# Moving the flips of the gate sums behind the next sums in a fused attention and mixture-of-experts kernel

## The chip, the cores and the metric

The kernel runs on one core of a Trainium2 chip. The metric is the device time of one execution in microseconds (us). The engines are named PE (TensorE, with its weight loads as PEld), DVE (VectorE), ACT (ScalarE), POOL (GpSimd) and SP (SyncE). Each takes its own queue in order.

## The reference

Attention over 8 batches, 12 heads, 448 tokens and 64 dimensions, with capped scores, and then a mixture of 8 experts with one expert for each token:

```python
scores = scale * np.matmul(q, k.transpose(0, 1, 3, 2))
scores = cap * np.tanh(scores / cap)
attn = np.exp(scores - max); attn = attn / (sum(attn) + 1e-09)
x = matmul(attn, v)                                   # 3584 tokens x 768
e_idx = np.argmax(x @ w_gate + modality_bias[modality_id], axis=1)
out[mask] = gate_w[mask, None] * (np.maximum(x[mask] @ w1[e], 0.0) @ w2[e])   # for each expert e
```

(The lines on the softmax and the experts are shortened.)

## The kernel before

The attention runs over 24 **units**, three to a batch; a unit is four heads of one batch. A unit has seven **steps** of 64 keys. The loop in `attention` goes over all 168 steps and writes the order of each engine by hand.

A step has on PE a group of eight score matmuls (L542, tile `sc`, two buffers) and a group of eight that weigh the values with an earlier step's probabilities (L574, tile `xT`, one buffer); each group works on four 64x64 tiles of the array. ACT takes the tanh of a step's scores (L547) and, after every second step, two exponentials (L549). So ACT's order is tanh, tanh, exp, exp. A scores group for step n writes the buffer that the tanh of step n-2 has read, so it waits for that tanh. DVE adds the probabilities up (L562, `tot`) and, once a unit's last step is weighed (which falls in step 3 of the next unit), copies `xT` out of PSUM (L581); the next unit's first weighing waits for that copy. It stands on PE in step 6 of an even unit and in step 5 of an odd unit, counted by the unit that is then being scored.

Two units, an even unit a and a+1, make a **pair**, and every 14 steps have some further work on PE for a pair:

- **sums** (`sums2`, L613 and L615, tile `glog`): softmax denominators and gate logits, sixteen recorded matmuls on 128x32 tiles of the array, in step 5 of an even unit; DVE copies them to `gl` (L619).
- **flip** (`turn2` calls `flip`, L604, tile `lt`): four 128x128 transposes of `gl`, in step 4 of the odd unit that follows, six steps after the sums; DVE then takes reciprocals (L632) into the batch's **payload** `pay`, and `logits` multiplies (L655).

When a batch's third unit has its logits, `start_route` begins its **route**: a chain of small DVE operations (L286 to L340), one small exponential on ACT, two small rank matmuls on PE, and then indirect DMAs from POOL (L346) that write payload rows to a map in DRAM. `go_on` moves a route on at given steps. The PE operations and the large DVE and ACT operations are pinned in the written order; most of the route's DVE operations aren't, and a scheduler places them. The payload of a batch has a buffer by its number modulo two.

After the loop come the closing sums and the experts' layers, in which PE multiplies almost without a break; their first expert needs the map, which is complete for all but the last batch some two units before the loop's end.

The lines that the change touches are in `payload` and `attention`:

Of the kernel before, what the change touches and what calls it, by code (L numbers as in the profile page):

```python
# [39 lines left out]
F32 = mybir.dt.float32  # L40
# [10 lines left out]
C, CP = 4, 112  # L51
# [13 lines left out]
ENTRY = 16  # L65
# [17 lines left out]
NU = NP // 2  # L83
ND = NU * B
PAIRED = ND - 4
LAGS = ((5, 5, 5, 5, 4, 4, 3), (6, 5, 5, 5, 4, 4, 4))
PLAGS = ((6, 6, 5, 5, 5, 4, 4), (5, 5, 5, 5, 4, 4, 4))
LAST = (4, 4, 4, 4, 4, 4, 4)
# [4 lines left out]
class Program:  # L93
# [7 lines left out]
    def pin(self, inst):  # L101
        return self.tc.keep_in_program_order(inst)
# [156 lines left out]
    def payload(self, b, pool, tok=None):  # L259

        nc = self.nc
        pay = pool.tile([CP, C, ENTRY], F32, name="pay" if tok is not None else f"pay{b % 2}")
        if tok is None:
            nc.gpsimd.memset(pay, 0.0)
            nc.gpsimd.iota(pay.bitcast(I32)[:, :, 0], pattern=[[CP, C]], base=b * S, channel_multiplier=1)
            nc.gpsimd.iota(
                pay[:, :, FOUR::SEG], pattern=[[Q * CP, C], [0, 2]], base=Q * b * S, channel_multiplier=Q,
                allow_small_or_imprecise_dtypes=True,
            )
        else:  # L270
            nc.gpsimd.memset(pay, 1.0)
            nc.vector.tensor_copy(pay.bitcast(I32)[:, :, 0], tok)
            for j in range(2):
                nc.vector.tensor_scalar(pay[:, :, FOUR + j * SEG], tok, float(Q), None, op0=ALU.mult)
        return pay
# [232 lines left out]
    def attention(self, firsts, rp, xp):  # L508
        tc, nc = self.tc, self.nc
        pe, pin, V = nc.tensor, self.pin, nc.vector  # L510
        with ExitStack() as st:
# [10 lines left out]
            def fetch(d):  # L522
                if d < ND:
                    for g in (2 * d, 2 * d + 1) if d else ():
                        self.load_kq(ring[g % 4], g)
                    vas[d] = ld.tile([128, VW], F32, name="va")
                    self.load(vas[d], self.v[d // NU, d % NU])
# [73 lines left out]
            def flip(gl, bank=None):  # L601
                bank = bank or self.ps_r.tile([128, 512], F32, name="lt", tag="small")
                for c in range(C):
                    pin(pe.transpose(bank[:CP, c * 128 : (c + 1) * 128], gl[:, c * CP : (c + 1) * CP], self.ident))  # L604
                return bank[:CP].rearrange("p (c g x) -> p c g x", c=C, g=4)

            def sums2(a, copy=V.tensor_copy):

                glog = self.glog = ps_g.tile([128, 512], F32, name="glog", tag="glog")
                group = lambda x: glog[x * GW : (x + 1) * GW, :S]  # L610
                every = [(u, g) for u in range(2) for g in range(2)]
                for u, g in every:
                    pin(pe.matmul(group(2 * u + g), self.pick2, tots[a + u][:, g], start=True, stop=False))  # L613
                for u, g in every:
                    pin(pe.matmul(  # L615
                        group(2 * u + g), self.wgt[:, (2 * (a + u) + g) % NP], kept[a + u][:, g], start=False, stop=True
                    ))
                gls[a] = xp.tile([128, S], F32, name="gl", bufs=2)
                pin(copy(gls[a], glog[:, :S]))  # L619

            def recs(d):

                b, r = divmod(d, NU)
                if r == 0:
                    pays[b] = self.payload(b, rp)
                return self.recips(pays[b])[:, :, :, 2 * r : 2 * r + 2]

            def turn2(a):

                lt = flip(gls.pop(a))  # L630
                for u in range(2):
                    pin(V.reciprocal(recs(a + u), lt[:, :, 2 * u : 2 * u + 2, GE : GE + 2]))  # L632
                    lts[a + u] = lt[:, :, 2 * u : 2 * u + 2]
# [12 lines left out]
            def logits(d):  # L646

                b, r = divmod(d, NU)
                lt = lts.pop(d)
                rec = self.recips(pays[b])  # L650
                if r == 0:
                    lgs[b] = xp.tile([CP, C, H, E], F32, name="lg", bufs=2)
                for i in range(2):
                    h0 = 4 * r + 2 * i
                    pin(V.tensor_tensor(  # L655
                        lgs[b][:, :, h0 : h0 + 2], lt[:, :, i, :GE].rearrange("p c (j e) -> p c j e", j=2),
                        rec[:, :, :, 2 * r + i].unsqueeze(3).to_broadcast([CP, C, 2, E]), op=ALU.mult,
                    ))
# [31 lines left out]
            def go_on():  # L690
                for way in routing:
                    next(way, None)
# [15 lines left out]
            for m in range(END):  # L708
                d, s = divmod(m, STEPS)
                due[min(m + (LAST if d == ND - 1 else (PLAGS if d < PAIRED else LAGS)[d % 2])[s], END)].append(m)  # L710
            added, held = 0, range(STEPS * (SOON + 2), STEPS * (SOON + 2) + 5)
# [12 lines left out]
            for n in range(END):  # L724
                d, s = divmod(n, STEPS)
                if s == 0:
                    fetch(d + 1)
                    if 1 < d < SOON and d % NU == 1:
                        store(d // NU - 1)
                    if d == 0:  # L730
                        self.fetch_bias()
                        self.fetch_cap()
                    if d == 1:
                        self.blank(xp.tile([128, FF], F32, name="spare", bufs=2))
                    if 0 <= d - 2 < CLEAR:
                        self.empty_map(d - 2)
                scores(n)
                late = False
                if not late:
                    more(n)  # L740
                if (d, s) == (1, 3):
                    self.gate_bias()
                if (d, s) == (1, 4):
                    self.columns()
                if s == 1 and d % 2 == 0 and self.rest:
                    self.rest.pop()()
                if s in ((1,), (1, 6))[d % 2] and d != SOON + 2:
                    go_on()
                if s == 4 and d % 2 and 3 <= d < PAIRED + 3:
                    turn2(d - 3)  # L750
                    go_on()
                    logits(d - 3)
                    logits(d - 2)
                if s == 5 and d % 2 == 0 and 2 <= d <= PAIRED:
                    sums2(d - 2)
                if (d, s) == (SOON + 1, 5):
                    sums(SOON)
                if s == 5 and d % 2 and 3 <= d < PAIRED + 2:
                    for u in (d - 3, d - 2):
                        if u % NU == NU - 1:  # L760
                            start_route(u // NU)
                if (d, s) == (SOON + 2, 2):
                    more(n, 1)
                for m in due[n]:
                    weigh(m)
                    if m % STEPS == STEPS - 1:
                        keep(m // STEPS)
                if s == 3 and d % 2 == 0 and d != SOON + 2:
                    go_on()
                if s == (2 if d % 2 else 4) and d % NU == 2:  # L770
                    tokens(d - 2)
                if s == (4 if d == SOON + 1 else 6) and 0 < d < ND - 1 and d % NU != 1:
                    tokens(d - 1)
                    if d == SOON + 1:
                        store(d // NU - 1)
                if d == SOON + 2 and s in (3, 4):
                    more(n, {3: 2, 4: 9}[s])
                if (d, s) == (SOON + 1, 6):
                    turn(SOON)
                    logits(SOON)  # L780
                    start_route(SOON // NU, firm=True)
                    go_on()
                    go_on()
                if (d, s) == (SOON + 2, 1):
                    go_on()
                    meta = self.early_slot(self.cpool, self.ps_r)
                    self.first_e = self.expert(meta, 0)
                    load_w1((0, 1), self.first_e)
                if (d, s) == (SOON + 2, 4):
                    maps = self.rows(meta, 0)  # L790
                    got = self.gather(maps, known=NT - S)
                    load_w1((2, 3, 4, 5), self.register(nc.gpsimd, meta[0:1, 0:1], E - 1, got.ins), nc.gpsimd)
                if d == SOON + 3 and s >= STEPS - TW:
                    self.norm(maps, s - (STEPS - TW))
# [818 lines left out]
```

## Time and profile before

| | us |
|---|---|
| median of 3 runs (lowest, highest) | 791.64 (791.25, 797.95) |
| the profiled execution, device time | 786.07 |
| its span, first to last instruction | 784.5 |
| mean granted TensorE clock of the span | 0.998 |

| engine | busy in the span |
|---|---|
| PE | 98% |
| DVE | 67% |
| ACT | 64% |
| POOL | 30% |

The busy shares are means over two very different stages. In the attention, which takes some 300 us, PE and ACT are both busy nearly all the time; in the experts' layers PE alone is. In the page's 40 slices ACT has a nine in slices 2 to 14, and three to six tenths from slice 17 to 39.

### The profile page before, as it was taken

How to read it: one execution, taken by the hardware profiler on the slowest of the kernel's cores; microseconds unless marked ns; L12 is line 12 of the kernel's file. 1: busy time of each engine (PE TensorE's matmuls, PEld its weight loads, DVE VectorE, ACT ScalarE, POOL GpSimd, SP SyncE). 2: the span in 40 equal slices, each digit the busy share in tenths (PEclk: the TensorE clock that was granted, in tenths of full speed). 3: DMA queues.
4: the chain of work that ended last, by engine and by line, in shares of the span. 5: the costliest groups of instructions: out<-in, count | busy, mean ns of one | idle time of the engine just before them, and what ended most of it. 6: DMA issues, size and time to landing. Idle time of an engine off the chain costs nothing. (4 is left out here: it accounts for less than half of the span.)

```text
span 784.5 us, 15421 instructions
## 1 busy us (share of the span) xinstructions
PE 772.2 (98%) x5811; PEld 580.0 (74%) x5811; DVE 524.3 (67%) x899; ACT 500.0 (64%) x704; POOL 238.4 (30%) x259
## 2 busy tenths in 40 slices
PE   7999999999999999999999999999999999999996
PEld 2343333343333337999999999999999999998985
DVE  4778897888798898965826448265482664727830
ACT  7999999999999895454533445235443354436630
POOL 3000121022122140248560723607427064015202
PEclk9999999999999999999999999999999999999999
DMA  6366545262544664598444563455634655346772
GB/s 201 115 205 204 163 144 182 102 213 94 192 141 146 165 219 154 141 311 277 157 138 176 191 229 131 142 202 185 201 124 157 228 174 183 109 176 207 244 283 98
DMA packets 58951, 139.33 MB, mean 178 GB/s; under 512 B 9025, under 2 KB 25814, under 8 KB 58867
## 3 DMA queue, kind: packets, MB, share of 16 engines
q1 hardware_dynamic: 48512, 113.32, 44.3%
q0 software_dynamic: 10352, 24.94, 9.4%
q8 instruction: 47, 0.77, 0.4%
q14 instruction: 38, 0.30, 0.1%
q10 hardware_dynamic: 2, 0.00, 0.0%
HBM read 114.47 MB, written 24.34 MB: 177 GB/s over the span
## 5 line engine op out<-in xcount | busy, mean ns | idle before, releaser
L549 ACT ACTIVATE pt<-pt 128x896 f32<-128x896 f32 x168 | 152.2, 972 | 0.0
L547 ACT ACTIVATE pt<-sc 128x896 f32<-128x896 f32 x164 | 145.6, 938 | 9.9 <-PE sc L542 9.6
L574 PE MATMUL xT<-pt,va 64*64 64x448 f32 x1344 | 149.8, 537 | 0.1
L1111 PE MATMUL py<-bh,hh 128*128 128x384 f32 (+1 forms) x440 | 147.9, 336 | 0.1
L1111 PE MATMUL py<-bh,hl 128*128 128x384 f32 (+1 forms) x440 | 147.5, 335 | 0.0
L1111 PE MATMUL py<-bl,hh 128*128 128x384 f32 (+1 forms) x440 | 147.5, 335 | 0.0
L1054 PE MATMUL ph<-x,al 128*128 128x384 f32 (+1 forms) x456 | 147.3, 323 | 0.0
L957 POOL DMA_INDIRECT xg<-xd,at x92 | 112.3, 1221 | 112.1 <-DVE look L1275 85.0
L562 DVE TENSOR_TENSOR tot<-tot,pt 128x896 f32<-128x896 f32 x118 | 127.8, 1083 | 9.2 <-ACT pt L549 3.4
L1050 PE MATMUL ph<-x,ah 128*128 128x384 f32 x360 | 120.6, 335 | 0.0
L1051 PE MATMUL ph<-x,ah 128*128 128x384 f32 x360 | 120.3, 334 | 0.0
L346 POOL DMA_INDIRECT mapd<-pay,pos x32 | 39.8, 1245 | 244.7 <-DVE pos L340 128.6
L574 PEld LDWEIGHTS xT<-pt,va 64*64 64x64 f32 x1344 | 51.1, 133 | 75.5 <-issue 70.8
L995 DVE TENSOR_TENSOR bl<-raw,bh 128x768 fp32r<-128x768 f32 x78 | 72.2, 955 | 39.8 <-ACT bh L994 39.5
L1133 ACT ACTIVATE ot<-py,mt 128x384 f32<-128x384 f32 (+1 forms) x55 | 31.9, 581 | 104.7 <-PE py L1111 93.8
L1054 PEld LDWEIGHTS ph<-x,al 128*128 128x128 f32 x456 | 85.7, 188 | 0.0
L1065 ACT ACTIVATE hh<-ph 128x384 fp32r<-128x384 f32 x63 | 30.6, 489 | 84.9 <-PE ph L1054 80.7
L1111 PEld LDWEIGHTS py<-bh,hh 128*128 128x128 f32 x440 | 82.6, 188 | 1.2 <-ACT ot L1133 0.5
L1111 PEld LDWEIGHTS py<-bl,hh 128*128 128x128 f32 x440 | 82.6, 188 | 0.3
L1111 PEld LDWEIGHTS py<-bh,hl 128*128 128x128 f32 x440 | 82.6, 188 | 0.3
L542 PE MATMUL sc<-kq 64*64 64x448 f32 x672 | 78.3, 551 | 4.0 <-ACT pt L547 4.0
L542 PE MATMUL sc<-kx 64*64 64x448 f32 x672 | 78.5, 540 | 0.1
(245 smaller groups left out, 972.9 us busy)
## 6 DMA issues: line engine op xcount, KB each, us to landing
raw<-in_w_dram SPq DMA_DIRECT2D x81, 384.0 KB, 4.7
raw<-in_w_dram SPq DMA_DIRECT2D x48, 512.0 KB, 4.5
va<-in_v_dram SPq DMA_DIRECT2D x24, 448.0 KB, 5.7
kx<-in_kq_dram SPq DMA_DIRECT2D x24, 448.0 KB, 3.8
xd<-xs SPq DMA_DIRECT2D x32, 336.0 KB, 6.8
kq<-in_kq_dram SPq DMA_DIRECT2D x22, 448.0 KB, 4.0
raw<-in_w1q_dram SPq DMA_DIRECT2D x12, 512.0 KB, 7.6
mapd<-spare SPq DMA_DIRECT2D x4, 480.0 KB, 8.1
```

What stands on the lines that cost most here:

```text
L346: put = nc.gpsimd.indirect_dma_start(self.mapd, bass.IndirectOffsetOnAxis(ap=pos, axis=0), pay[:, c, :], None, bounds_check=E * RG - 1, oo ...
L542: pin(pe.matmul(sc[i * KB : (i + 1) * KB, j, :S], kq[rows, S + s * KB : S + (s + 1) * KB], kq[rows, :S], start=True, stop=True,))
L547: pin(nc.scalar.activation(weights(n), sc[:, :, :S], AF.Tanh, scale=self.isc if slow else self.iscr))
L549: pin(nc.scalar.activation(weights(m), weights(m), AF.Exp, scale=self.cabsr))
L562: pin(V.tensor_tensor(tots[d], pt_of(n - 1) if s == 1 else tots[d], pt_of(n), op=ALU.add))
L574: pin(pe.matmul(self.xT[j * D : (j + 1) * D, i, :S], vas[d][rows, o : o + D], pt[rows, j], start=s == 0, stop=s == STEPS - 1,))
L957: got = self.nc.gpsimd.indirect_dma_start(self.xg.rearrange("p t f -> p (t f)")[:, g * QW : (g + 1) * QW], None, self.xd.rearrange("n (q c ...
L995: keep((minus or self.nc.vector).tensor_tensor(lo, raw, hi, op=ALU.subtract))
L1050: keep(nc.tensor.matmul(ph[:, :w], hi[:, fs], self.x[:, k, 0, :w], start=first, stop=False))
L1051: keep(nc.tensor.matmul(ph[:, :w], hi[:, fs], self.x[:, k, 1, :w], start=False, stop=False))
L1054: self.done = keep(nc.tensor.matmul(ph[:, :w], lo[:, fs], self.x[:, k, 0, :w], start=False, stop=last)).ins
L1111: got = nc.tensor.matmul(pys[half][:, :wide], self.h[a][:, f, rows], self.w2s[f][c][:, cs], start=f == i == 0, stop=f == FC - 1 and i == 2,)
```

## The change

Units below `SOLO` = 14, the pairs that begin at units 0, 2, ..., 12, get another place for the flip: no longer in step 4 of the odd unit after their sums, but in step 5 of the next even unit, directly behind the sums of the next pair. Their reciprocals and logits go with it. The three pairs from unit 14 on keep their place. A route of a batch that ends in a pair below `SOLO` (batches 0 to 3) starts two units later; the others start where they did. The payload has three buffers in turn instead of two.

```diff
+SOLO = PAIRED - 6
...
-        pay = pool.tile([CP, C, ENTRY], F32, name="pay" if tok is not None else f"pay{b % 2}")
+        pay = pool.tile([CP, C, ENTRY], F32, name="pay" if tok is not None else f"pay{b % 3}")
...
                 if s == 4 and d % 2 and 3 <= d < PAIRED + 3:
-                    turn2(d - 3)
+                    if d - 3 >= SOLO:
+                        turn2(d - 3)
                     go_on()
-                    logits(d - 3)
-                    logits(d - 2)
+                    if d - 3 >= SOLO:
+                        logits(d - 3)
+                        logits(d - 2)
                 if s == 5 and d % 2 == 0 and 2 <= d <= PAIRED:
                     sums2(d - 2)
+                    if 0 <= d - 4 < SOLO:
+                        turn2(d - 4)
+                        logits(d - 4)
+                        logits(d - 3)
...
-                if s == 5 and d % 2 and 3 <= d < PAIRED + 2:
-                    for u in (d - 3, d - 2):
+                if s == 5 and d % 2 and 5 <= d < PAIRED + 2:
+                    a = d - 3 if d - 3 >= SOLO else d - 5
+                    for u in (a, a + 1):
                         if u % NU == NU - 1:
                             start_route(u // NU)
```

In the changed program the lines after the new one are numbered one higher up to the loop (L542 becomes L543, L604 becomes L605).

On PE in an odd unit, around step 4, the program before has these rows (a row `sc` x4 is the scores group of one step, `xT` x4 the weighing of one step, `lt` the flip):

```order
L542 MATMUL sc<-kx 64x448 x4
L574 MATMUL xT<-pt,va 64x448 x8
L542 MATMUL sc<-kx 64x448 x4
L574 MATMUL xT<-pt,va 64x448 x4
L542 MATMUL sc<-kx 64x448 x4
L604 MATMUL lt<-ident,gl 112x128 x4
L542 MATMUL sc<-kx 64x448 x4
L574 MATMUL xT<-pt,va 64x448 x4
```

The changed program has there:

```order
L543 MATMUL sc<-kx 64x448 x4
L575 MATMUL xT<-pt,va 64x448 x8
L543 MATMUL sc<-kx 64x448 x4
L575 MATMUL xT<-pt,va 64x448 x4
L543 MATMUL sc<-kx 64x448 x8
L575 MATMUL xT<-pt,va 64x448 x4
```

The flip is gone from between the scores of steps 4 and 5, which now follow each other. On PE around the sums of an even unit, the changed program has these rows (before, the `lt` row isn't there):

```order
L543 MATMUL sc<-kq 64x448 x8
L614 MATMUL glog<-tot,pick_99 32x448 x4
L616 MATMUL glog<-xT,wgt 32x448 x4
L605 MATMUL lt<-ident,gl 112x128 x4
L543 MATMUL sc<-kq 64x448 x4
L575 MATMUL xT<-pt,va 64x448 x4
```

The flip stands between the last sum and the scores of step 6. On DVE in the odd unit in which batch 2's route begins in the changed program, the rows ahead of the copy of `xT` are (L563 is the addition, L582 the copy, the others belong to the route):

```order
L563 TENSOR_TENSOR tot<-tot,pt 128x896
L290 TENSOR_TENSOR L<-L,bias 112x32
L563 TENSOR_TENSOR tot<-tot,pt 128x896
L295 TENSOR_REDUCE mx<-L 112x4
L563 TENSOR_TENSOR tot<-tot,pt 128x896
L296 TENSOR_TENSOR L<-L,mx 112x32
L308 SCALAR_TENSOR_TENSOR sc<-L,desc 112x32
L312 TENSOR_REDUCE first<-sc 112x4
L314 TENSOR_TENSOR oh<-sc,first 112x32
L320 TENSOR_TENSOR before<-before,oh 112x8 x3
L321 TENSOR_TENSOR acc<-before,oh 112x8
L582 COPY xT<-xT 128x896
```

Before, in the odd unit in which that batch's route begins, the same operations begin only behind the copy:

```order
L581 COPY xT<-xT 128x896
L632 RECIPROCAL pay_1330<-lt 112x4x2x2
L632 RECIPROCAL pay_1559<-lt 112x4x2x2
L655 TENSOR_TENSOR lg<-lt,pay_1330 112x4x16 x2
L655 TENSOR_TENSOR lg<-lt,pay_1559 112x4x16 x2
L562 TENSOR_TENSOR tot<-pt 128x896
L286 TENSOR_REDUCE L<-lg 112x32
L289 TENSOR_TENSOR L<-L,bias 112x32
L562 TENSOR_TENSOR tot<-tot,pt 128x896
L294 TENSOR_REDUCE mx<-L 112x4
L295 TENSOR_TENSOR L<-L,mx 112x32
L307 SCALAR_TENSOR_TENSOR sc<-L,desc 112x32
```

So the copy that the next unit's weighing waits for moves from ahead of the route's first operations to behind them, in the four odd units that begin the routes of batches 0 to 3.

## Rows read from the trace of the kernel before

**Rows 1.** The page: span, and busy time of each engine.

```profile
span 784.5 us, 15421 instructions
PE 772.2 (98%) x5811; PEld 580.0 (74%) x5811; DVE 524.3 (67%) x899; ACT 500.0 (64%) x704; POOL 238.4 (30%) x259
```

**Rows 2.** Busy time of one pair's stretch: length, PE, PEld, DVE, ACT, POOL, clock, DMA.

```profile
122.86:146.46 23.60, 23.60 (x249) 9.11 (x248) 18.54 (x27) 23.24 (x29) 2.14 (x4) 1.00 0.57 177
```

**Rows 3.** Waits of PE: who waited for whom, total us, times, longest.

```profile
PE sc L542 <- ACT pt L547: 4.0, 4, 1.5
```

**Rows 4.** PE in order of time, sums of an even unit (start us, length us).

```profile
132.02 0.94 PE L615 MATMUL glog<-xT,wgt 128*32 128x448 f32 x8
132.88 0.98 PE L542 MATMUL sc<-kq 64*64 64x448 f32 x8
...
134.44 0.93 PE L542 MATMUL sc<-kx 64*64 64x448 f32 x8
```

**Rows 5.** PE in order of time, flip in the odd unit that follows.

```profile
141.96 0.93 PE L542 MATMUL sc<-kx 64*64 64x448 f32 x8
142.82 0.65 PE L604 MATMUL lt<-ident,gl 128*112 128x128 f32 x4
143.40 0.98 PE L542 MATMUL sc<-kx 64*64 64x448 f32 x8
144.20 0.93 PE L574 MATMUL xT<-pt,va 64*64 64x448 f32 x8
...
146.46 0.56 PE L542 MATMUL sc<-kq 64*64 64x448 f32 x4
```

**Rows 6.** ACT in order of time, same units; in brackets idle time before, and releaser.

```profile
134.95 1.78 ACT L547 ACTIVATE pt<-sc 128x896 f32<-128x896 f32 x2
...
142.96 0.92 ACT L547 ACTIVATE pt<-sc 128x896 f32<-128x896 f32 x1 [0.36 <-PE sc L542]
143.77 1.79 ACT L549 ACTIVATE pt<-pt 128x896 f32<-128x896 f32 x2
145.45 1.71 ACT L547 ACTIVATE pt<-sc 128x896 f32<-128x896 f32 x2
```

**Rows 7.** PE in order of time, start of unit 2: no flip stands before it.

```profile
26.36 0.93 PE L574 MATMUL xT<-pt,va 64*64 64x448 f32 x8
27.70 0.98 PE L542 MATMUL sc<-kq 64*64 64x448 f32 x8 [0.42 <-ACT pt L547]
```

**Rows 8.** PE in order of time, behind the loop: transposes directly after sums.

```profile
293.92 0.94 PE L615 MATMUL glog<-xT,wgt 128*32 128x448 f32 x8
294.79 0.55 PE L1011 MATMUL ptr<-ident,xg 128*128 128x128 f32 x3
295.26 0.98 PE L574 MATMUL xT<-pt,va 64*64 64x448 f32 x8
```

**Rows 9.** DVE in order of time, odd unit 11, route of batch 2 beginning.

```profile
133.56 4.67 DVE L562 TENSOR_TENSOR tot<-tot,pt 128x896 f32<-128x896 f32 x4
...
142.21 1.09 DVE L581 COPY xT<-xT 128x896 f32<-128x896 f32 x1 [1.97 <-PE xT L574]
143.51 0.46 DVE L632 RECIPROCAL pay<-lt 112x16 f32<-112x16 f32 x2 [0.21 <-PE lt L604]
...
144.36 1.08 DVE L562 TENSOR_TENSOR tot<-pt 128x896 f32<-128x896 f32 x1
145.35 0.86 DVE L286 TENSOR_REDUCE L<-lg 112x32 f32<-112x384 f32 x1
...
146.36 1.08 DVE L562 TENSOR_TENSOR tot<-tot,pt 128x896 f32<-128x896 f32 x1
147.36 0.18 DVE L294 TENSOR_REDUCE mx<-L 112x4 f32<-112x32 f32 x1
...
148.36 1.10 DVE L665 STREAM_TRANSPOSE xs<-xT 128x896 f32<-128x896 f32 x1
```

**Rows 10.** The line of the map's DMAs: from issue to landing.

```profile
DMA to landing us min/median/max: 2.1/5.4/7.8
```

**Rows 11.** Busy time by stretch: the loop's start, where PE waits for ACT.

```profile
8.00:16.00 8.00, 4.97 (x49) 1.44 (x48) 3.47 (x4) 8.00 (x11) 0.00 (x0) 1.00 0.39 140
```

## The prediction

> **What bounds the kernel now.** I read the page first. Its span [rows 1] has PE busy for 98%, so a change in the attention shows in the time only through PE: what PE loses there, the experts' layers, in which PE is busy almost throughout, don't give back. The reader should not stop at that row, since in the attention a second engine is nearly as full. The stretch of one pair, units 10 and 11, is 23.60 us long; PE is busy for 23.60 and ACT for 23.24 [rows 2]. So ACT has 0.36 us to spare in a pair, and PE nothing that the view shows. The waits of PE come next: in the whole attention PE waits for ACT four times, 4.0 us in all [rows 3], and none of these is in the regular pairs.
>
> Then I read, in order of time, where each engine leads the other. In the odd unit PE does the scores of step 4 at 141.96, the flip at 142.82 and the scores of step 5 at 143.40 [rows 5]. ACT waits there, for 0.36 us, until 142.96, for the scores that began at 141.96 [rows 6]: this is the pair's one ACT wait, and ACT follows PE. From there ACT runs without a pause: tanh at 142.96, two exponentials, the next two tanh from 145.45. The first of these frees the buffer for the scores of the next even unit. It lasts about 0.92, as the tanh at 142.96 does, so it ends at 146.37, and those scores begin at 146.46 [rows 5]. So there PE follows ACT, with only 0.09 us between the tanh's end and the start. PE would gain nothing by coming earlier.
>
> Hence the pair's period is a loop over two engines: PE's work from the even unit's first scores to the odd unit's scores of step 4 (122.86 to 141.96 is 19.10 us), the handover to ACT (1.00, 141.96 to 142.96), ACT's work up to 146.37 (3.41) and the handover back (0.09). The sum is 23.60, the pair's length [rows 2]. The flip lies outside the loop: it is done while PE would wait for ACT anyway. The sums lie inside it.
>
> The trace has one place that shows this without the flip. Unit 1 has none in its step 4, and at the start of unit 2 PE does wait for ACT: the scores begin 1.34 us after the weighing ahead of them instead of the usual 0.75, with 0.42 us shown as idle [rows 7].
>
> **The change part by part.** *The flip taken out of the odd unit.* From the scores at 141.96 to those at 143.40 is 1.44 us, and without a flip two groups start 0.75 apart (144.20 less 143.40 is 0.80, with 0.05 for the first group after a flip) [rows 5]. So it frees 0.69, and 0.74 with that 0.05. All of it lies ahead of the scores at 146.46, which can't begin more than the 0.09 earlier. I take the gain as 0; its bounds are 0 and 0.09 a pair.
>
> *The flip put behind the sums.* From the last sums to the next scores is now 0.86 (132.02 to 132.88) [rows 4]. With a flip between, it is one switch from sums to transposes and then the flip. Transposes directly behind sums do occur, after the loop: sums to transposes 0.87, so the same as sums to scores, and from three transposes to the next group 0.47 [rows 8]. Four of them with the way back are 0.58 (142.82 to 143.40) [rows 5]. So the insertion costs the 0.58, between 0.44 (four times the 0.11 by which 0.58 and 0.47 differ, no switch) and 0.69 (a further switch of 0.11). I take 0.58, measured for this very flip.
>
> It lies inside the loop. Behind the sums ACT has work left: its tanh for the scores at 132.88 begins at 134.95 only [rows 6], 1.1 us after these scores end, so ACT doesn't notice the delay at once. From the next scores on (134.44 [rows 4]) it does, and at step 4 of the odd unit ACT is as late as PE: 0.58. Everything after it, up to the next even unit's scores, is late by 0.58 too. Then the next pair begins so.
>
> *The sum.* Seven pairs are moved (units 0 to 12 by twos): 7 times 0.58 is 4.06, less 0 to 0.63 for the handover. The pair would be 24.18 us long where PE's own work falls from 23.60 to 23.44, since 0.74 leaves and 0.58 comes; PE then waits about 0.7 us at each even unit's first scores, as at unit 2.
>
> [...]
>
> *Reciprocals and logits on DVE.* They take 0.85 us (143.51 to 144.36) [rows 9] and move with the flip, to behind the copy of the sums. Nothing of the pair's PE work waits for them. They cost nothing as long as the copy of `xT` in the odd unit keeps its time: ahead of it DVE is idle for 1.97 [rows 9].
>
> *The routes.* Batches 0 to 3 begin two units later, and by the order their first operations now stand ahead of that copy. These take 1.01 us (145.35 to 146.36, L286 and L289) and 1.00 (147.36 to 148.36) [rows 9], and four more small ones at 0.18 to 0.23 each, 0.9 at most: 2.9. With the 0.85 that is 3.75, against 1.97 idle time and the 0.58 by which PE is later: the copy is up to 1.2 us late. Less is likelier: four additions in a row take 4.67, 1.16 each, where one with other work behind it takes 1.01 [rows 9], so operations between additions fill some 0.15 each; that makes 0.6. What waits is PE's first weighing of the odd unit (144.20 [rows 5]). Without the flip ahead it comes 0.16 earlier than now while the copy comes 0.58 later, which leaves 0.16 of the present 0.9 between the copy's end (143.30) and it. But PE has 0.7 to wait for ACT two steps later, and a late copy uses that up first. So 0.8 is covered: I take 0, and at the upper end 0.4 for each of four routes, 1.6 us.
>
> *Three payload buffers.* A refill waits for the DMAs of three batches earlier to land. The tightest is batch 5's, behind batch 2's last DMA in step 1 of unit 16, needed in step 4 of unit 17: ten steps of 1.69 us (23.60 over 14), against at most 7.8 us to landing [rows 10]. It costs nothing. The last map rows before the experts (batches 4 to 6) keep their place.
>
> **Rivals.** *Not slower: the switch counts.* If PE didn't follow ACT at the even unit, PE's work alone would set the time: 7 times 0.16 is 1.1 us faster, 785.0 on the profiled execution, 790.5 by the median. For it speaks the row that has PE busy for all of the pair; against it the 0.09 between tanh and scores, and unit 2. *No change:* the freed time and the inserted time cancel because ACT's 0.36 and its lead behind the sums take the delay up; within 0.5 us of 791.6. The lead is against it: it is used up before step 4, where ACT waits already.
>
> *Much slower: the copy.* If it came 1.8 us late or more at the four routes (0.6 more than the bound above), PE would lose 1.0 or more at each beyond the 0.8 that is covered, 4 us beside the forecast's 4: from there the change is over 1% slower, 799.7.
>
> [...]
>
> **How the numbers follow.** The forecast is made on the profiled execution: its 786.07 (span 784.5 and 1.6 around it) plus 4.06 is 790.1. That execution is 5.6 us, 0.7%, below the median of the three runs, 791.64; by the median it is **795.7**. Its own range is 794.1 (0.44 a pair less the 0.09) to 798.1 (0.69 a pair, 4.8, and the 1.6 of the copy). Chances: forecast 0.75, switch rival 0.10, no change 0.07, copy 0.05, clock 0.03. The range reaches down to the switch rival, 790.0, and up to 799.0, since the runs' own spread goes more above the median (to 797.95) than below it. A measurement of this kernel can tell about 1% from no change, 7.9 us; the forecast is half of that. So within 1% gets 0.91, slower 0.07 (copy, clock), and faster 0.02, for which no case here has the size.
>
> **What would show it.** Right, if in the changed profile a moved pair without rank work is 24.1 to 24.2 us long, PE waits for ACT about 0.7 us at each even unit's first scores from unit 4 to 16, ACT waits longer than 0.36 in the pair, and pairs from unit 18 on are as before. The insertion is mis-sized if sums to scores isn't 0.86 plus 0.58. The loop is wrong if pairs are 23.44 and PE doesn't wait. The route is wrong if PE waits for the copy of `xT` at first weighings of units 7, 9, 13 and 15.

## The result, and the profile after

| | before | changed |
|---|---|---|
| median of 11 runs each, us | 791.25 | 794.04 |
| lowest, highest | 788.02, 797.95 | 791.57, 800.64 |
| span of the profiled execution | 784.5 | 789.7 |

The ratio of the times is 1.0058, with a 95% interval of 1.0030 to 1.0086: the changed kernel is 4.6 us slower (2.4 to 6.8). The medians are 2.8 us apart. The prediction had 4.06 us.

The profiled spans differ by 5.2 us. Of these, 0.50 lie ahead of unit 4 (the start differs by more between two executions of the changed kernel: 51.84 and, in its repetition, 50.38), 4.55 between the starts of units 4 and 18, where the seven moved flips now stand, and 0.16 behind. The page of the changed kernel:

```profile
span 789.7 us, 15428 instructions
PE 774.5 (98%) x5811; PEld 579.9 (73%) x5811; DVE 525.2 (67%) x899; ACT 501.9 (64%) x704; POOL 234.7 (30%) x259
```

Nothing stands out here against [rows 1]: PE is at 98% in both. The change is visible only in the attention. Busy time by stretch (length, PE, PEld, DVE, ACT, POOL, clock, DMA), first of the kernel before, units 4 to 17:

```profile
51.34:217.97 166.63, 166.63 (x1720) 64.02 (x1720) 140.71 (x244) 163.18 (x201) 22.33 (x28) 1.00 0.51 165
```

And of the changed kernel: units 4 to 17, then the pair of units 4 and 5, then the pair of units 8 and 9, in which a route begins.

```profile
51.84:223.02 171.18, 168.63 (x1720) 63.99 (x1724) 141.07 (x248) 163.93 (x201) 17.38 (x24) 1.00 0.50 160
51.84:76.01 24.17, 23.66 (x245) 9.04 (x245) 18.34 (x24) 23.37 (x29) 0.00 (x0) 1.00 0.68 212
100.18:124.72 24.54, 24.18 (x246) 9.08 (x246) 21.45 (x43) 23.56 (x30) 3.27 (x3) 1.00 0.34 115
```

The pair is 24.17 us long where it was 23.60 [rows 2]. PE is no longer busy in all of it: 0.51 us are idle. A pair with a route's two rank matmuls is 24.54; before it was 23.96. The waits of PE between 30 and 262 us, which had no entry at all before, are now these (total us, times, longest):

```profile
PE sc L543 <- ACT pt L548: 2.2, 5, 0.7
PE xT L575 <- DVE xT L582: 0.7, 2, 0.4
```

PE of the changed kernel in order of time (start us, length us, in brackets the idle time and who ended it): the sums of unit 4 with the flip behind them, the start of unit 6, and the first weighing of unit 9.

```profile
61.04 0.93 PE L616 MATMUL glog<-xT,wgt 128*32 128x448 f32 x8
61.91 0.65 PE L605 MATMUL lt<-ident,gl 128*112 128x128 f32 x4
62.48 0.98 PE L543 MATMUL sc<-kq 64*64 64x448 f32 x8
...
74.56 0.93 PE L575 MATMUL xT<-pt,va 64*64 64x448 f32 x8
76.01 0.98 PE L543 MATMUL sc<-kq 64*64 64x448 f32 x8 [0.51 <-ACT pt L548]
...
120.27 1.68 PE L543 MATMUL sc<-kx 64*64 64x448 f32 x16
122.31 0.98 PE L575 MATMUL xT<-pt,va 64*64 64x448 f32 x8 [0.36 <-DVE xT L582]
123.11 0.93 PE L543 MATMUL sc<-kx 64*64 64x448 f32 x8
123.87 0.93 PE L575 MATMUL xT<-pt,va 64*64 64x448 f32 x8
124.72 0.98 PE L543 MATMUL sc<-kq 64*64 64x448 f32 x8
```

DVE in unit 9, where the copy of `xT` now stands behind the route's first operations:

```profile
121.09 0.16 DVE L321 TENSOR_TENSOR acc<-before,oh 112x8 bf16<-112x8 bf16 x1
121.17 1.08 DVE L582 COPY xT<-xT 128x896 f32<-128x896 f32 x1
```

From the last sums to the scores are 1.44 us (61.04 to 62.48), where [rows 4] has 0.86: the insertion is 0.58, as taken. At 76.01 the even unit's first scores begin 1.45 after the weighing ahead of them instead of 0.75: PE waits 0.70 for ACT. In unit 9 it waits for the copy of `xT` first: two scores groups take 1.50, so the weighing could begin at 121.77 and begins at 122.31, 0.54 late. Three groups on, at 124.72, only 0.10 is left of the wait for ACT (0.85 less 0.75). So the wait for ACT isn't the same at every even unit: it is 0.70 at units 4 and 6, 0.43 at units 8 and 14, and 0.1 at units 10 and 16; at unit 12 it is 0.23.

ACT of the changed kernel in order of time, in units 5 and 11:

```profile
68.80 0.92 ACT L548 ACTIVATE pt<-sc 128x896 f32<-128x896 f32 x1 [0.36 <-PE sc L543]
69.61 1.78 ACT L550 ACTIVATE pt<-pt 128x896 f32<-128x896 f32 x2
71.29 0.91 ACT L548 ACTIVATE pt<-sc 128x896 f32<-128x896 f32 x1
72.55 0.92 ACT L548 ACTIVATE pt<-sc 128x896 f32<-128x896 f32 x1 [0.36 <-PE sc L543]
73.37 1.78 ACT L550 ACTIVATE pt<-pt 128x896 f32<-128x896 f32 x2
75.05 1.72 ACT L548 ACTIVATE pt<-sc 128x896 f32<-128x896 f32 x2
...
139.10 1.78 ACT L550 ACTIVATE pt<-pt 128x896 f32<-128x896 f32 x2
142.17 1.73 ACT L548 ACTIVATE pt<-sc 128x896 f32<-128x896 f32 x2 [1.29 <-PE sc L543]
```

In a pair without rank matmuls ACT waited for scores once [rows 6]. Now it waits twice (68.80 and 72.55), 0.36 each time: it is late by the flip. From 72.55 on it runs without a pause, up to the tanh for which the scores at 76.01 wait. The last line is a pause of 1.29 us of another kind, which comes up below.

### The profile page after: what moved, and what is told of

Its sections match the earlier page's. It is cut to its first block, busy times and chain, and to the rows that moved or that the text cites. A ratio compares the mean times of both kernels' runs of the same rounds, so it can differ in the third digit from the quotient of the medians.

```text
span 789.7 us, 15428 instructions
## 1 busy us (share of the span) xinstructions
PE 774.5 (98%) x5811; PEld 579.9 (73%) x5811; DVE 525.2 (67%) x899; ACT 501.9 (64%) x704; POOL 234.7 (30%) x259
## 3 DMA queue, kind: packets, MB, share of 16 engines
HBM read 114.47 MB, written 24.34 MB: 176 GB/s over the span
## 5 line engine op out<-in xcount | busy, mean ns | idle before, releaser
L563 DVE TENSOR_TENSOR tot<-tot,pt 128x896 f32<-128x896 f32 x118 | 127.8, 1083 | 9.0 <-ACT pt L550 3.4
L347 POOL DMA_INDIRECT mapd<-pay,pos x32 | 36.3, 1134 | 252.0 <-DVE pos L341 131.3
L543 PE MATMUL sc<-kq 64*64 64x448 f32 x672 | 79.1, 557 | 6.2 <-ACT pt L548 4.9
L543 PE MATMUL sc<-kx 64*64 64x448 f32 x672 | 77.1, 538 | 1.1 <-ACT pt L548 1.0
```

What stands on the lines that cost most here:

```text
L347: put = nc.gpsimd.indirect_dma_start(self.mapd, bass.IndirectOffsetOnAxis(ap=pos, axis=0), pay[:, c, :], None, bounds_check=E * RG - 1, oo ...
L543: pin(pe.matmul(sc[i * KB : (i + 1) * KB, j, :S], kq[rows, S + s * KB : S + (s + 1) * KB], kq[rows, :S], start=True, stop=True,))
L563: pin(V.tensor_tensor(tots[d], pt_of(n - 1) if s == 1 else tots[d], pt_of(n), op=ALU.add))
```

## The experiments

The times of runs scatter by some 10 us. Pairs of one kind in a trace agree within 0.05, but for the pair at unit 10 in two traces (25.00 and 24.75 in the table). So each kernel is judged by its pair lengths, from the first scores of an even unit to those of the next even unit, beside its time. The lengths come from one trace of each kernel, and from two of the changed one. Pairs with a route's rank matmuls are some 0.36 longer in every kernel; in the kernels with later routes (the changed ones and the one with the flip two units later) these are the pairs at units 8, 10, 14 and 16, in the others those at 6, 8, 12 and 14. In this order the pairs begin at units 2, 4, ..., 16:

| | 2 | 4 | 6 | 8 | 10 | 12 | 14 | 16 |
|---|---|---|---|---|---|---|---|---|
| before | 23.64 | 23.59 | 23.96 | 23.96 | 23.60 | 23.96 | 23.96 | 23.60 |
| changed | 23.59 | 24.17 | 24.18 | 24.54 | 25.00 | 24.17 | 24.54 | 24.58 |
| changed, again | 23.59 | 24.17 | 24.17 | 24.54 | 24.54 | 24.17 | 24.54 | 24.58 |
| flip two units later, old place | 23.59 | 23.64 | 23.59 | 23.96 | 23.96 | 23.60 | 23.96 | 25.75 |
| changed, and a spare flip | 23.64 | 24.18 | 24.17 | 24.54 | 24.75 | 24.22 | 24.54 | 24.54 |
| before, flip in step 2 | 24.34 | 26.09 | 25.41 | 24.65 | 26.11 | 25.43 | 24.65 | 23.64 |
| before, light exponentials | 23.59 | 23.59 | 23.96 | 23.96 | 23.59 | 23.96 | 23.95 | 23.59 |
| changed, light exponentials | 22.85 | 23.43 | 23.69 | 24.37 | 23.79 | 23.69 | 24.38 | 24.53 |
| before, flip in step 5 | 23.64 | 23.60 | 23.96 | 23.96 | 23.59 | 23.96 | 23.96 | 23.59 |
| before, flip done twice | 24.34 | 24.30 | 24.66 | 24.66 | 24.30 | 24.66 | 24.66 | 23.59 |

**The changed kernel once more**, with no edit.

> The changed kernel once more, as it is, profiled and timed. Its profile showed six of the seven moved pairs at the lengths that the loop over PE and ACT gives (24.17 us without rank work), and one, units 10 and 11, 0.46 us longer, with one ACT wait of 1.29 us in unit 11. Loop theory: that wait is a chance of the one execution; the pair comes back at 24.5 us (24.17 and 0.37 of rank work), the other pairs are the same within 0.03, and the time is 0.5% (4.1 us) above before. Rival (the wait belongs to the change, from the later route of batch 1): it comes back in the same place, and the pair is 25.0 us again.

Measured: 791.89 us against 788.93 of before in the same series, ratio 1.0024 (0.9996 to 1.0053). That is 1.9 us by the ratio (from 0.3 faster to 4.2 slower), half of the 0.5% expected, and the interval includes no change. So the times alone don't settle the size; the trace does better. Busy time by stretch of this execution, units 4 to 17 and the pair of units 10 and 11:

```profile
50.38:221.10 170.72, 168.49 (x1720) 63.95 (x1722) 141.00 (x248) 163.77 (x201) 17.67 (x24) 1.00 0.50 161
123.27:147.81 24.54, 24.11 (x251) 9.16 (x247) 19.95 (x33) 23.38 (x30) 4.56 (x7) 1.00 0.55 173
```

The seven pairs are 4.09 us longer than before (170.72 against 166.63), the prediction's 4.06. The 25.00 of the pair at unit 10 didn't come back: here it is 24.54.

**Only the routes later.** The flips stay in the odd unit's step 4, but two units later, with their reciprocals and logits. The routes start when they do in the changed kernel, and the payload has its three buffers. The edit against the changed kernel, shortened, with the three calls put on one line:

```
 if s == 4 and d % 2 and 3 <= d < PAIRED + 3:
+    if 0 <= d - 5 < SOLO:
+        turn2(d - 5); logits(d - 5); logits(d - 4)
 ...
 if s == 5 and d % 2 == 0 and 2 <= d <= PAIRED:
     sums2(d - 2)
-    if 0 <= d - 4 < SOLO:
-    ...
```

> Routes two units later and three payload buffers as in the changed kernel, but the flips stand in step 4 of an odd unit (two units later than before) and not behind the sums. Loop theory: the flip is done while PE would wait for ACT anyway, so pairs are as before (23.60 without rank work) and the time is that of before, within 0.5 us. Rival (the later routes, their DVE work ahead of the copy or the payload buffers cost the time): about 0.5% above before, as the changed kernel is, with PE waits at the copy.

Measured: 790.28 against 788.93, ratio 0.9998 (0.9960 to 1.0036). The pairs that begin at units 12, 14 and 16 by stretch, and PE's longest wait between 30 and 262 us:

```profile
146.65:170.25 23.60, 23.60 (x249) 9.09 (x248) 18.56 (x27) 23.24 (x29) 2.09 (x4) 1.00 0.57 177
170.25:194.21 23.96, 23.96 (x251) 9.17 (x250) 21.47 (x43) 23.38 (x30) 3.56 (x3) 1.00 0.34 118
194.21:219.95 25.74, 24.58 (x254) 9.68 (x254) 22.10 (x50) 23.86 (x30) 5.00 (x7) 1.00 0.56 163
```

```profile
PE lt L605 <- DVE lg L656: 1.2, 1, 1.2
```

Later routes and three buffers cost nothing here: every pair up to unit 15 is as long as one of its kind before, 23.6 without rank matmuls and 23.96 with them. This doesn't test the route's operations ahead of the copy: in this variant the copy of `xT` in unit 7 (94.48) comes ahead of the reciprocals (95.78), the logits (96.07) and the route's first operation (97.61), as before. The pair at unit 16 is this variant's own doing: in unit 17 two flips follow each other through the one buffer of `lt`, and the second waits 1.2 us for the first one's logits. So the time of this variant doesn't settle much; its pairs do.

**A spare flip where the old one was**, beside the moved one.

```
                     if d - 3 >= SOLO:
                         turn2(d - 3)
+                    else:
+                        flip(gls[d - 3])
```

> The changed kernel with an extra flip of the same sums in its old place, step 4 of the odd unit, for the seven moved pairs; its result isn't used. PE does 0.74 us more in each. Loop theory: it falls into PE's wait of 0.69 for ACT, so pairs stay at 24.17 to 24.2, that wait all but vanishes, and the time is that of the changed kernel within 0.5 us (0.5% above before). Rival (PE's own work sets the time): seven times 0.74, 5.2 us above the changed kernel, 1.2% above before.

Measured: 793.28 against 788.93, ratio 1.0068 (1.0033 to 1.0104). The median is 1.4 above that of the changed kernel in the same series, where 0.5 at most was expected, within the scatter of the runs. By stretch, units 4 to 17 and the pair of units 4 and 5:

```profile
50.96:221.91 170.95, 170.92 (x1749) 66.83 (x1748) 140.97 (x248) 163.92 (x201) 17.93 (x24) 1.00 0.50 161
50.96:75.14 24.18, 24.18 (x253) 9.53 (x252) 18.34 (x25) 23.38 (x29) 0.00 (x0) 1.00 0.69 213
```

There are six more flips in this stretch (the seventh is in unit 3), and PE is busy for 2.4 us more than in the repetition above (170.92 against 168.49). But the stretch is only 0.23 longer, of which 0.21 is the one pair at unit 10, and a pair is 24.18 as without them. PE's waits between 30 and 262 us are gone from the view. So what the removal had freed was indeed worth nothing: PE only waits in it.

**The flip in step 2 of the odd unit**, in the kernel before: inside the loop, with no other change in PE's work; seven pairs.

```
-                if s == 4 and d % 2 and 3 <= d < PAIRED + 3:
+                if s == 2 and d % 2 and 3 <= d < PAIRED - 3:
                     turn2(d - 3)
```

(Its logits move with it, and the last pairs keep step 4.)

> The kernel before with the flips of the same seven pairs moved two steps up, from step 4 to step 2 of the same odd unit; PE's work, routes and payloads are as before. Loop theory: the flip then lies ahead of the scores of step 4 that ACT waits for, inside the loop, so each moved pair is 0.74 longer (24.33 without rank work) and the time 5.2 us, 0.65%, above before. Rival (what costs in the changed kernel is the flip's place right behind the sums, or the routes): no change, pairs of 23.60.

Measured: 799.36 against 788.93, ratio 1.0129 (1.0068 to 1.0190). The first four pairs by stretch, PE's longest wait, and the place of it in order of time:

```profile
27.93:52.27 24.34, 23.82 (x245) 9.04 (x245) 18.91 (x24) 23.35 (x29) 0.00 (x0) 1.00 0.48 157
52.27:78.35 26.08, 23.86 (x244) 9.13 (x248) 20.14 (x35) 23.77 (x29) 0.00 (x0) 1.00 0.61 196
78.35:103.76 25.41, 24.18 (x250) 9.16 (x246) 21.51 (x43) 23.73 (x30) 4.56 (x3) 1.00 0.50 165
103.76:128.41 24.65, 24.14 (x250) 9.07 (x242) 20.35 (x33) 23.31 (x30) 5.27 (x7) 1.00 0.36 117
```

```profile
PE xT L574 <- DVE xT L581: 6.9, 4, 2.2
```

```profile
72.15 1.68 PE L542 MATMUL sc<-kx 64*64 64x448 f32 x16
76.05 0.98 PE L574 MATMUL xT<-pt,va 64*64 64x448 f32 x8 [2.21 <-DVE xT L581]
```

The pairs in which no route begins are 0.69 or 0.70 longer (0.74 was expected): here, too, a flip inside the loop costs its own length. The four others are 1.45 to 2.51 longer, which wasn't expected (10.0 us in all instead of 5.2). There logits and the route's first operations stand together ahead of the copy of `xT`; on DVE the route's first and the copy are

```profile
72.02 0.84 DVE L286 TENSOR_REDUCE L<-lg 112x32 f32<-112x384 f32 x1
...
74.91 1.08 DVE L581 COPY xT<-xT 128x896 f32<-128x896 f32 x1
```

The weighing could begin at 73.65 and begins at 76.05, 2.40 late, and the 0.7 that PE has to wait for ACT anyway doesn't cover that. This is the prediction's "copy" rival, at a place where it does happen.

**Light exponentials**, in both kernels: ACT takes the exponentials over 128 of 448 columns only, so that ACT isn't near its limit. The sums and the routing have other values then, and the experts' layers take longer; only the attention's pairs are compared.

```
-    pin(nc.scalar.activation(weights(m), weights(m), AF.Exp, scale=self.cabsr))
+    few = weights(m)[:, :, :128]
+    pin(nc.scalar.activation(few, few, AF.Exp, scale=self.cabsr))
```

> The kernel before, with the exponentials of the attention taken over 128 of the 448 columns only (the others keep the tanh), so that ACT has less to do; the output is another, and the experts get other token counts, so the experts' layers may take another time. It is the base for the next run. Loop theory: PE's own work set the pair's length already, so pairs stay at 23.60 us without rank work and 23.96 with it, and PE gets room ahead of the even unit's first scores: the two exponentials between the tanh that follows the odd unit's step 4 and the next tanh shrink from 0.84 each to about 0.3. Rival (ACT's total work sets the pair): pairs get shorter.

> The changed kernel with the same exponentials left out (128 of 448 columns). Loop theory: ACT's part of the loop is about 1.1 us shorter, more than the 0.58 that the flip adds to PE's part, so PE doesn't wait at the even unit's first scores and PE's own work sets the pair: 23.44 us without rank work and 23.80 with it, 0.16 a pair shorter than the run before it, the opposite sign of the change at full exponentials. Rival (the flip costs its 0.58 behind the sums whatever ACT does, or the routes cost it): 24.17 and 24.54, as with full exponentials.

Measured: 1192.81 us for before, 1190.18 for the changed kernel. By stretch, before with light exponentials, the pairs at units 4 and 10:

```profile
47.84:71.43 23.59, 23.59 (x248) 9.19 (x244) 18.49 (x26) 16.89 (x29) 0.00 (x0) 1.00 0.69 218
119.34:142.93 23.59, 23.59 (x248) 9.19 (x244) 18.54 (x27) 16.89 (x29) 2.14 (x4) 1.00 0.56 177
```

And the changed kernel with light exponentials, the pairs at units 4 and 8, with PE's waits between 30 and 262 us:

```profile
46.86:70.29 23.43, 23.43 (x249) 9.24 (x245) 18.34 (x24) 16.76 (x29) 0.00 (x0) 1.00 0.70 220
93.97:118.35 24.38, 24.03 (x251) 9.27 (x247) 21.67 (x43) 16.90 (x30) 3.27 (x3) 1.00 0.34 116
```

```profile
PE xT L576 <- DVE xT L583: 0.7, 2, 0.4
```

With ACT at 16.9 us, before keeps its 23.59: PE's own work is a limit as long as the loop. The changed kernel's pair, though, falls to 23.43: where no route begins, the change saves 0.16 with a light ACT and has the other sign. In the pair at unit 2, where a flip is taken out and none put in, it is 0.74 shorter (22.85). Both are the prediction's numbers for PE's work. The four pairs in which a route begins were expected at 23.44 and 23.80 and took 23.69 and 24.37: here the wait for the copy (0.26 and 0.57) has no wait for ACT behind it that would cover it, and shows in full. The four together lose some 1.7, more than the 1.1 (seven times 0.16) by which PE's work falls: over all eight pairs of the table the changed kernel is still 0.54 longer (190.73 against 190.19).

**The flip in step 5**, one group later, in the kernel before (edit as for step 2, with `s == 5`).

> The kernel before with the flips of the same seven pairs moved one step down, to step 5 of the odd unit, behind that step's scores. Loop theory: that is still after the scores of step 4 that ACT waits for and before the next even unit's first scores, so the flip stays hidden: pairs of 23.60 and 23.96, the time of before within 0.5 us. Rival (step 4 is the one place that hides it): longer pairs, up to 0.7 each.

Measured: 788.41 against 789.83, ratio 0.9970 (0.9934 to 1.0006). By stretch, units 4 to 17:

```profile
50.47:217.10 166.63, 166.63 (x1721) 63.40 (x1720) 139.51 (x243) 163.25 (x201) 23.36 (x28) 1.00 0.51 165
```

The stretch is as long as in the kernel before, to 0.01 us. So step 4 isn't the one place that hides the flip: behind the scores of step 5 it is hidden as well, as the loop has it. Later places weren't tried.

**The flip done twice**, in the kernel before, step 4.

```
+                    if d - 3 < PAIRED - 6:
+                        flip(gls[d - 3])
                     turn2(d - 3)
```

> The kernel before with the flip in step 4 of the odd unit done twice for the same seven pairs (the first result isn't used), four transposes of 0.11 us more on PE, without a switch. Loop theory: the time that PE has to spare there is filled by one flip (0.09 us is left between the tanh's end and the even unit's first scores), so the second costs 0.35 to 0.43 in each of the seven pairs: 23.95 to 24.03 without rank work, 2.5 to 3.0 us in all, 0.3 to 0.4%. Rival (there is more room for PE in that stretch, since ACT is the later engine): pairs of 23.60, no change.

Measured: 792.57 against 787.23, ratio 1.0074 (1.0057 to 1.0090). PE in order of time around the two flips:

```profile
71.33 0.93 PE L542 MATMUL sc<-kx 64*64 64x448 f32 x8
72.19 1.35 PE L604 MATMUL lt<-ident,gl 128*112 128x128 f32 x8
73.48 0.98 PE L542 MATMUL sc<-kx 64*64 64x448 f32 x8
```

The second flip took 0.71 (72.19 to 73.48 is 1.29, less 0.58), not the 0.44 of four transposes at 0.11 from which the expectation started, and all but 0.01 of it shows: each of the seven pairs is 0.70 longer. The hidden stretch holds one flip and has no room beyond it.

## Why the prediction was right

- **The loop over PE and ACT** was right. The pair grew by 0.57 to 0.58, and PE waits at the even unit's first scores, though for 0.70 only at two of them, where the prediction named about 0.7 at each. Its two opposite tests agree: the spare flip costs nothing in the freed place, and a flip put at another place inside the loop (step 2) costs its 0.70. With a light ACT the cost turns into a gain of 0.16 in pairs in which no route begins, so there it hangs on ACT being full and not on PE's work.
- **The gain of the removal, 0,** was right: 0.74 is freed (22.85 against 23.59 with a light ACT) and PE waits 0.70 instead at units 4 and 6, and for ACT and the copy together elsewhere.
- **The insertion, 0.58 each,** was right in the rows (1.44 against 0.86) and in the sum: 4.09 over seven pairs in the repetition, against 4.06. In the first profile the seven pairs add to 4.55; 0.46 of that is the one pair at unit 10. The times agree with the sum only loosely: 4.6 us in the first series and 1.9 in the second, each give or take 2.2. The measured median, 794.04, lies 1.7 below the 795.7: 0.4 of that is the median of before (791.25 over eleven runs, 791.64 over the first three), and the rest is within the scatter.
- **The routes, 0,** were right in the sum, though the sign named for it was badly chosen. The text said the route is wrong if PE waits for the copy of `xT` at the first weighings of units 7, 9, 13 and 15. It does, by 0.22 and 0.54 in turn (units 7 and 13, units 9 and 15). But the wait for ACT three groups on shrinks by as much, as the working had it with its 0.8 of cover: the pairs at units 6, 8, 12 and 14 are 24.18, 24.54, 24.17 and 24.54, which is what pairs without a route's start take (24.17, and 24.54 with rank work). What should have been named is a pair's length. The runs with light exponentials and with step 2 show the cost where the cover is gone or too small.
- **The payload buffers, 0,** were right: the variant with later routes and three buffers has the pairs of before.
- **The switch rival** (0.16 a pair faster) had the right size for PE's work and the wrong limit: the 0.16 appears only with a light ACT (23.43 against 23.59), and with the full ACT it doesn't decide the time (24.17 against 23.60). That the 0.16 is a switch saved was the author's reading of the starts: 0.86 from sums to scores [rows 4] against 0.75 between like groups, which is also the "further switch of 0.11". What the 0.16 consists of is not shown by a run.
- **The clock rival** (0.03) fell: the granted clock is 1.00 in each pair's stretch of the changed kernel, although PE waits at each of the even units 4 to 16. That added waits could lower it was the author's guess. In the kernel before, PE was busy for 4.97 of 8 us at the loop's start with the clock at 1.00 [rows 11], and in no stretch shown here is it below that.

One thing stays open: the pause of ACT of 1.29 us at 142.17 in the first profile. The view names PE's scores as what ended it, and those of this tanh began at 139.55 and had ended by their record 1.7 us before it. But the trace also records when the semaphore was raised that the tanh waits for: at 142.15, 2.60 after the scores began, where 0.97 is the median of that trace. So PE's signal came late, and the view is right. In unit 11 ACT paused in the repetition (first line) and in the kernel with the spare flip (second line), too:

```profile
137.39 0.92 ACT L548 ACTIVATE pt<-sc 128x896 f32<-128x896 f32 x1 [0.89 <-PE sc L543]
...
138.56 0.92 ACT L548 ACTIVATE pt<-sc 128x896 f32<-128x896 f32 x1 [1.52 <-PE sc L543]
```

These pauses are 0.53 and 1.16 longer than the usual 0.36; the pair lost nothing in the first case and 0.21 in the second. Between 28 and 250 us the first trace of the changed kernel has three signals that come more than 1.1 after their scores began (2.60, 1.91 and 1.12), that of the kernel before none; the one of 1.91, in unit 17, left its pair at 24.58, as it is in the repetition. So the 0.46 isn't part of every execution. Why PE signals late, and whether the moved flip makes it likelier, isn't shown.

## What to carry to other kernels

Where two engines that hand work to each other are both nearly full, write the period as a loop over both, and ask of each instruction whether it lies inside the loop or in the part where its engine waits anyway. Here, moving the flip from there into the loop cost its whole length, 0.57 to 0.58 a pair, even though PE's own work got 0.16 shorter. A wait that appears in the profile can be taken back by a later wait on the same engine, as the 0.22 and 0.54 for the copy of `xT` were here: judge by the length of the period.

## What was not expected of the hardware

A second flip directly behind the first, with no change of tiling between them (both are on 128x112), takes 0.71 us. That is as much as a single flip costs with its change of tiling from 64x64 and back (0.69, which is 1.44 less 0.75 in [rows 5]), although the second one needs no change. The weight loads of the double-flip kernel in order of time show where it goes:

```profile
72.19 0.41 PEld L604 LDWEIGHTS lt<-ident,gl 128*112 128x112 f32 x4 [0.70 <-issue]
72.90 0.40 PEld L604 LDWEIGHTS lt<-ident,gl 128*112 128x112 f32 x4 [0.30 <-PE lt L604]
```

Both flips write the one buffer of `lt`, and the second's first weight load waits 0.30 us for the first's transposes to end. So of the 0.71, 0.30 is this wait, and 0.41 is left for four transposes. That the shared buffer is what makes the second flip wait is likely, not shown: a kernel with two buffers wasn't tried.
